# Six instead of three expert layers by seven products of quarters, with sums and copies in another order

## The chip, the core and the metric

The kernel runs on one core of a Trainium2 chip. A core has the engines PE (TensorE, matmul, with its weight loads as PEld), DVE (VectorE), ACT (ScalarE), POOL (GpSimd) and SP (SyncE, which only issues transfers here); sixteen DMA engines move data between HBM and SBUF. The metric is the time of one execution on the device, in microseconds. Each engine runs its own instructions in the order in which the program lists them.

## The reference

An attention with decay is followed by a mixture of experts in which a token may stick to its predecessor's expert. 8 batches of 576 tokens have 512 features; 8 experts have 1024 hidden features.

```python
def _attn_ref(q, k, v, f):
    scores = scale * np.matmul(q, k.transpose(0, 1, 3, 2))
    cum = np.cumsum(np.log(np.clip(f, 0.0001, 1.0)), axis=-1)
    scores = np.where(causal, -1000000000.0, scores + (cum[:, :, :, None] - cum[:, :, None, :]))
    attn = np.exp(scores - np.max(scores, axis=-1, keepdims=True))
    return np.matmul(attn / (np.sum(attn, axis=-1, keepdims=True) + 1e-09), v)
...
def _moe_ref(x, w_gate, w_local, w1, w2):
    logits = np.einsum('bsd,de->bse', x, w_gate)
    local_gate = 1.0 / (1.0 + np.exp(-np.einsum('bsd,de->bse', x, w_local).squeeze(-1)))
    for b in range(B):
        prev_e = -1
        for s in range(S):
            fresh_e = int(np.argmax(logits[b, s]))
            e = fresh_e if s == 0 or local_gate[b, s] < 0.5 else (prev_e if prev_e >= 0 else fresh_e)
            prev_e = e
            p = softmax(logits[b, s])
            out[b, s] = p[e] * (np.maximum(x[b, s] @ w1[e], 0.0) @ w2[e])
```

## The kernel before

The first 440 us are attention and routing, which the change leaves alone up to where the experts begin. Then each expert's tokens are gathered and the expert's two layers run over them. Two experts (0 and 1) are fixed and have run a part of their tokens by then; `fixed` runs their remainder of 256 and 320 tokens. Six more are *ranked* by their number of tokens, so that their rooms have fixed sizes of 608, 592, 576, 576, 544 and 480 tokens (`RANKC`), and `ranked` runs them one after the other. Which expert has which rank is known only on the chip, so its weights are loaded through a register.

All products are f16 in three parts: a value is cut into a high half (ACT, `uh`, `wh`, `hh`, `th`) and a low rest (DVE, `ul`, `wl`, `hl`, `tl`), and high x high, high x low and low x high are added up in PSUM. Cutting a ready tile is therefore one ACT and one DVE instruction (L2093, L2094). The hidden activations are cut in the ReLU itself: ACT writes `hh`, DVE writes `hl` from the same source and `hh`.

A **plain first layer** has 8 column blocks of 12 products, each in two halves of the tokens: 192 matmuls of n = tokens/2 columns (z, L1763), and per block one ReLU of all tokens on ACT (L1738) and its low part on DVE (L1739), both from PSUM.

A first layer **by sevens** (`seven`) splits the 512 input rows and the 1024 hidden columns into quarters of the weights and the tokens into halves, and forms the four blocks of the result from seven products of sums instead of eight. That is 28 products of 6 matmuls of n columns (L1848), 168 in all, in four groups g; a generator yields after each product. It needs the sums of quarters of the weights: POOL adds and subtracts f32 tiles (`add` L2117, `subtract` L2122, two times `less` L2131 for each half c of the rows, eight operations of 512 columns), and ACT and DVE cut the results (`second_row`, `differences`, `first_row`, each 1024 wide, `total` 512 wide, for both c). It needs sums of the token halves: `sums_of` makes them on DVE from the transposed tokens `xT` and cuts them (`part` and `cut`, L1908 to L1922). In the layer itself the products 1, 6 and 7 share one PSUM bank (`zb`), so ACT copies its state out after each (`kept`, L1855); DVE adds such a copy to another product (L1861), and ACT and DVE make the ReLU of the sum (L1863, L1864). The product after must wait for the copy before it overwrites the bank. In the last group the order is 1, 2, 4, 6, 5, 7, 3, 4, 3, where the first 4 and 3 belong to the group before.

A **second layer** has 24 products of 512 columns for each tile of 128 tokens (L1805, L1809); ACT scales the result (`put`, L1749) and POOL scatters it to `out` (L1751).

What stands beside these is a list `todo` of calls with step numbers: `run` issues each call after that step of the current expert (steps 0 to 27 are the products of a layer by sevens, or the half blocks of a plain one's 16, and four steps for each tile of the second layer follow). During expert r the list prepares expert r + 1: `load` (SP, 512 KB weight tiles into a ring of seven), gathers of tokens (POOL, L1695) and their transposes (SP, L1700), quarter sums, cuts, token sums. Before the change the second, fourth and sixth ranked expert go by sevens and are prepared during the first, third and fifth, which are plain and have 16 steps in the first layer (`SA`, `SB`, `LA`, `UA`, `TA`, `XA`); the plain ones are prepared beside layers by sevens (`XB`, `UB`, `PB`):

```python
                todo += [(16, free), (XA[0], both(*gs)), (XA[1], both(*ts))]
                for name, at in (SA if r < 4 else SB).items():
                    todo += [call(at[c], getattr(N, name), c) for c in C2]
                todo += [call(LA[2 * c + h], N.less, c, h) for c in C2 for h in C2]
                todo += [(TA[j], N.parts[j]) for j in range(4)]
                todo += [call(UA[j], N.second, j, None) for j in range(4)]
```

## Time and profile before

| | us |
|---|---|
| median of 3 runs | 782.54 (781.16 to 785.14) |
| the profiled execution | 784.0 |
| its span | 782.3 |
| busy: PE, PEld | 743.6, 542.0 |
| busy: DVE, ACT, POOL | 541.9, 477.0, 437.9 |
| mean granted clock | 0.993 |

The profile is of one execution. A window lists the busy time of each engine in a stretch with the number of its instructions, the granted clock as a share of full speed (1.00 is 2.4 GHz), and the share of DMA time. A group of instructions has a line of the program, an engine, an operation and its shape; then its count, its busy time in us, the mean of one in ns, and the engine's idle time before with what ended it. A time line lists an engine's instructions by their start in us and length in us; in brackets the idle time before it and the releaser.

### The profile page before, as it was taken

The page shows a single profiled execution, that of the slowest core. Times are in us where ns is not written, and L with a number is a line of the kernel's source. Part 1 is how long each engine was busy: PE and PEld are TensorE (multiplying, and loading weights), DVE is VectorE, ACT ScalarE, POOL GpSimd, SP SyncE. Part 2 cuts the span into 40 slices and gives each one's busy share as a digit, 9 for nine tenths or more (in the row PEclk, how much of TensorE's full clock was granted, in tenths as well). Part 3 has the DMA queues.
Part 4 walks back from the last instruction along what each step waited for, and adds up shares of the span by engine and source line. Part 5 has one row for each costly group of instructions (what it writes and reads, how often), then busy time and mean ns, then how long its engine had stood idle before and what let it go on. Part 6 is the DMA issues. An engine that isn't in the chain of part 4 may idle for free.

```text
span 782.3 us, 21826 instructions
## 1 busy us (share of the span) xinstructions
PE 743.6 (95%) x8733; PEld 542.0 (69%) x8733; DVE 541.9 (69%) x1211; ACT 477.0 (61%) x922; POOL 437.9 (56%) x497
## 2 busy tenths in 40 slices
PE   6898999999999998989799999999999999999996
PEld 3686888887778877877555576675665747476682
DVE  6886888898898989899758845166462574637440
ACT  7886788988878878868633334244463544525431
POOL 6879969395779859838692424181311924155101
PEclk9999999999999999999999999999999999999999
DMA  7569879698786868155794765939357293656101
GB/s 190 134 132 213 168 160 186 158 155 202 157 188 124 176 154 158 34 102 189 175 259 169 224 137 135 263 81 223 130 109 250 68 292 107 129 203 142 42 2 52
DMA packets 189659, 120.76 MB, mean 154 GB/s; under 512 B 129397, under 2 KB 165511, under 8 KB 189532
## 3 DMA queue, kind: packets, MB, share of 16 engines
q1 hardware_dynamic: 183473, 100.19, 55.1%
q0 software_dynamic: 6080, 19.13, 8.3%
q8 instruction: 70, 1.15, 0.6%
q14 instruction: 36, 0.29, 0.1%
HBM read 72.25 MB, written 19.32 MB: 117 GB/s over the span
## 4 chain that ended last, share of the span: by engine, by line
PE 65%; DVE 11%; issue 9%; ACT 6%; POOL 4%; DMA 3%; POOLq 1%; ACTq 0%; DVEq 0%
PE y L1805 17%; PE z L1763 12%; PE pt L940 8%; PE st L894 7%; PE xp L919 6%; DVE nm L905 4%; PE zb L1848 3%; PE st L429 3%; DVE pl L949 3%; ACT P L925 2%; ACT ph L945 2%; PE zd L1848 2%; POOLq L1750 1%; PE st L901 1%; PE y L1809 1%
## 5 line engine op out<-in xcount | busy, mean ns | idle before, releaser
L925 ACT ACTIVATE P<-st,nm 128x512 f32<-128x512 f32 (+3 forms) x288 | 152.8, 588 | 28.0 <-DVE nm L905 26.0
L905 DVE TENSOR_REDUCE nm<-st 128x1 f32<-128x512 f32 (+4 forms) x264 | 133.4, 542 | 8.0 <-PE st L901 5.5
L945 ACT CAST ph<-pt 128x512 f16<-128x512 f32 (+1 forms) x200 | 115.3, 587 | 35.3 <-PE pt L940 32.8
L940 PE MATMUL pt<-ident,P 128*128 128x128 f32 x784 | 121.0, 280 | 4.9 <-DVE pl L949 2.1
L949 DVE TENSOR_TENSOR pl<-pt,ph 128x512 f16<-128x512 f32 (+1 forms) x165 | 109.1, 669 | 22.6 <-ACT ph L945 20.8
L1751 POOL DMA_INDIRECT out_dram<-o,ranki x26 | 28.9, 1111 | 163.8 <-ACT o L1749 96.1
L1763 PE MATMUL z<-xT,wh 128*128 128x384 f16 (+5 forms) x640 | 117.8, 294 | 0.1
L1805 PE MATMUL y<-uh,hh 128*128 128x512 f16 x264 | 100.2, 379 | 0.0
L1805 PE MATMUL y<-uh,hl 128*128 128x512 f16 x264 | 100.2, 379 | 0.0
L1805 PE MATMUL y<-ul,hh 128*128 128x512 f16 x264 | 100.2, 379 | 0.0
L940 PEld LDWEIGHTS pt<-ident,P 128*128 128x128 f32 x784 | 83.8, 142 | 21.2 <-DVE pl L949 3.7
L919 PE MATMUL xp<-VH,pl 128*128 128x65 f16 (+1 forms) x960 | 89.2, 194 | 5.8 <-DVE pl L949 5.1
L919 PE MATMUL xp<-VH,ph 128*128 128x65 f16 (+1 forms) x960 | 90.8, 195 | 2.0 <-ACT ph L945 2.0
L1805 PEld LDWEIGHTS <-hh 128*128 128x128 f16 x528 | 51.3, 98 | 58.6
L919 PEld LDWEIGHTS <-ph 128*128 128x128 f16 (+1 forms) x1920 | 83.0, 102 | 10.4 <-issue 3.3
L919 PE MATMUL xp<-VL,ph 128*128 128x65 f16 (+1 forms) x960 | 90.2, 194 | 0.0
L1739 DVE SCALAR_TENSOR_TENSOR hl<-z,hh 128x384 f16<-128x384 f32 (+5 forms) x56 | 34.0, 611 | 75.2 <-ACT hh L1738 75.1
L894 PE MATMUL st<-Ak,Aq 128*128 128x256 f16 (+4 forms) x448 | 78.1, 285 | 4.4 <-ACT P L925 2.4
L894 PE MATMUL st<-KB,QB 70*128 70x256 f16 (+4 forms) x448 | 77.6, 282 | 2.0 <-DMA KB<-Ak 2.0
L919 PEld LDWEIGHTS <-pl 128*128 128x128 f16 (+1 forms) x960 | 74.7, 102 | 7.1 <-DVE pl L949 6.2
L1763 PE MATMUL z<-xT,wl 128*128 128x384 f16 (+5 forms) x320 | 78.5, 294 | 0.0
L1763 PEld LDWEIGHTS <-wh 128*128 128x128 f16 x640 | 61.9, 98 | 22.3 <-issue 0.7
(415 smaller groups left out, 1594.2 us busy)
## 6 DMA issues: line engine op xcount, KB each, us to landing
stg<-in_moe_w_dram SPq DMA_DIRECT2D x64, 512.0 KB
xs<-xr SPq DMA_DIRECT2D x16, 512.0 KB
ldq<-in_q_dram SPq DMA_DIRECT2D x14, 512.0 KB
ldk<-in_k_dram SPq DMA_DIRECT2D x14, 512.0 KB
ldv<-in_v_dram SPq DMA_DIRECT2D x28, 256.0 KB
QB<-Aq SPq DMA_DIRECT2D x15, 256.0 KB
KB<-Ak SPq DMA_DIRECT2D x15, 256.0 KB
ldv<-in_v_dram SPq DMA_DIRECT2D x20, 64.0 KB
```

What stands on the lines that cost most here:

```text
L894: nc.tensor.matmul(st[p0:p0 + m, co:co + n], lhsT=queries(lq, kk, h, c), rhs=rhs, start=(ps == 0 and first and co == col), stop=(ps == 1), ...
L905: nc.vector.tensor_reduce(dst, src, axis=AX.X, op=ALU.max, negate=True)
L919: nc.tensor.matmul(xo, lhsT=a[:, c0:c0 + m], rhs=w[:, vi, :], start=False, stop=(i == n - 1 and jj == 2), skip_group_check=True)
L925: nc.scalar.activation(P[:, c0:c1].rearrange("p (k x r) -> p k r x", r=2, x=64), st[:, c0:c1].rearrange("p (k r x) -> p k r x", r=2, x=64) ...
L940: nc.tensor.matmul(U["pt"][:, i * 128:(i + 1) * 128], lhsT=P[:, i * 128:(i + 1) * 128], rhs=ident, is_transpose=True, start=(i == 0), stop ...
L945: nc.scalar.copy(U["ph"][:, :cols], U["pt"][:, :cols])
L949: nc.vector.tensor_tensor(U["pl"][:, :cols], U["pt"][:, :cols], U["ph"][:, :cols], ALU.subtract)
L1739: nc.vector.scalar_tensor_tensor(lv, z[:, 0:nh, 0:wd], 0.0, hv, ALU.max, ALU.subtract)
L1751: nc.gpsimd.indirect_dma_start(out=outf if EX.get("over") else next_out(), out_offset=bass.IndirectOffsetOnAxis(ap=scat(t)[0:m], axis=0), ...
L1763: nc.tensor.matmul(z[:, a, 0:wd], lhsT=w[:, d, fc * 128:(fc + 1) * 128], rhs=xT[:, x, a * wd:(a + 1) * wd], start=(i == 0), stop=(i == len ...
L1805: nc.tensor.matmul(y[0:m], lhsT=a[:, fc, t * 128:t * 128 + m], rhs=u[:, fc], start=(i == 0), stop=(i == len(prods) - 1))
L1848: nc.tensor.matmul(out, lhsT=w, rhs=v, start=(start and i == 0), stop=(i == len(ops) - 1), skip_group_check=True)
```

## The change

All six ranked experts now have their first layer by sevens; there is no plain one left beyond the fixed experts. PE has 72 matmuls and as many weight loads less on its list. What prepares an expert is laid out anew, the same for each r. In the first layer of expert r stand the gathers (step 4), then the eight sums of quarters on POOL (steps 6 to 13), three of four pairs of cuts of expert r's own second-layer weights (`UC`, six high cuts on ACT and six low ones on DVE, 512 wide), the transposes (step 20) behind a load (`UN`, step 18). In its second layer stand all cuts of quarters (`WC`) and the token sums (`TA`) of the next expert, and at step 45 the first quarter of its second-layer weights (`UB`). The first ranked expert is prepared during the two fixed ones (`FA`). `sums_of` works on all four blocks of a half at once, in operations of 4n, 2n, n and n elements, and cuts 4n at once. In `seven` the ReLU of a sum is put off (`later`) behind the next product's copy. `less` writes to a new tile `s3` instead of the loaded weights. The first layer's quarters live in `wpa` alone; `wpb` and the freed halves of it hold the second layer's weights in turn; the pool `ov` goes, its tiles lie in rooms of `fx`. The core of the diff:

```diff
-SA = {"add": (2, 7), "subtract": (3, 8), "second_row": (4, 9), "differences": (10, 14), "first_row": (20, 22), "total": (24, 25)}
-SB = {**SA, "differences": (14, 18)}
...
+SEVEN = (1, 1, 1, 1, 1, 1)
+WP = (28, 30, 32, 36)
+LA = (6, 7, 8, 9), (10, 11, 12, 13)
+UC = (0, 1), (2, 3), (8, 10), (15, 17), (22, 23), (26, 27)
+UB = 45
+UN = (5, 18, 28)
+XA = (4, 20)
+WC = (28, 29, 29, 30, 31, 31, 38, 38)
+TA = (28, 36, 37, 44)
+FA = (9, 10, 11, 12, 13, 14, 15, 16), (17, 18, 19, 20), (1, 4, 7, 9), (17, 22), (15, 16, 17, 18), 22
...
-            return EX["fx"].tile([128, 304], F32, name="et", bufs=7)[:, 0:n]
+            return EX["fx"].tile([128, 304], F32, name="et", bufs=5)[:, 0:n]
...
-            nc.scalar.activation(hh[:, fc, half[h]], x, AF.Relu)
-            nc.vector.scalar_tensor_tensor(hl[:, fc, half[h]], x, 0.0, hh[:, fc, half[h]], ALU.max, ALU.subtract)
+
+            def finish():
+                nc.scalar.activation(hh[:, fc, half[h]], x, AF.Relu)
+                nc.vector.scalar_tensor_tensor(hl[:, fc, half[h]], x, 0.0, hh[:, fc, half[h]], ALU.max, ALU.subtract)
+
+            if plus is None:
+                finish()
+            else:
+                later.append(finish)
+
+        later = []
...
+            while len(later) > (p in (2, 3, 7)):
+                later.pop(0)()
...
+            if p == last[-1]:
+                for f in later:
+                    f()
...
-            x = [[EX["fx"].tile([128, 304], F32, name="et", bufs=7)[:, 0:n] for h in range(2)] for d in range(2)]
-            for d in range(2):
-                for h in range(2):
-                    y = slice(h * n, h * n + n)
-                    nc.vector.tensor_tensor(x[d][h], xT[:, 2 * d + c, y], xT[:, 4 + 2 * d + c, y], ALU.add)
-            (b11, b12), (b21, b22) = x
-            nc.vector.tensor_tensor(b11, b12, b11, ALU.subtract)
-            nc.vector.tensor_tensor(b12, b22, b12, ALU.subtract)
-            nc.vector.tensor_tensor(b22, b22, b11, ALU.subtract)
-            nc.vector.tensor_tensor(b21, b21, b22, ALU.subtract)
-            S_[c] = x
+            x = S_[c] = EX["fx"].tile([128, 2, 2, 304], F32, name="sx", bufs=1)[:, :, :, 0:n]
+            whole = [xT[:, i:i + 3:2, 0:2 * n].rearrange("p d (h x) -> p d h x", h=2) for i in (c, 4 + c)]
+            nc.vector.tensor_tensor(x, *whole, ALU.add)
+            flat = x.rearrange("p d h x -> p (d h) x")
+            nc.vector.tensor_tensor(flat[:, 0:2], flat[:, 1:4:2], flat[:, 0:2], ALU.subtract)
+            nc.vector.tensor_tensor(x[:, 1, 1], x[:, 1, 1], x[:, 0, 0], ALU.subtract)
+            nc.vector.tensor_tensor(x[:, 1, 0], x[:, 1, 0], x[:, 1, 1], ALU.subtract)
 
         def cut(c):
             x = S_.pop(c)
-            for d in range(2):
-                for h in range(2):
-                    y = slice(h * n, h * n + n)
-                    nc.scalar.copy(th[:, c, d, y], x[d][h])
-                    nc.vector.tensor_tensor(tl[:, c, d, y], x[d][h], th[:, c, d, y], ALU.subtract)
+            hi, lo = (t[:, c, :, 0:2 * n].rearrange("p d (h x) -> p d h x", h=2) for t in (th, tl))
+            nc.scalar.copy(hi, x)
+            nc.vector.tensor_tensor(lo, x, hi, ALU.subtract)
...
+        def second_room(self, r):
+            names, to = (("wh", "wl"), "p d (h m) -> p (d h) m") if r % 2 == 0 else (("uh", "ul"), "p (d h) m -> p (d h) m")
+            self.u = [EX["wpb"].tile([128, NF, DM] if r % 2 else [128, ND, FF], F16, name=x).rearrange(to, h=2) for x in names]
+
+        def second(self, j, c, low):
+            hi, lo = (x[:, 2 * j + c] for x in self.u)
+            t = self.ts[ND + j].rearrange("p (c m) -> p c m", c=2)[:, c]
+            if not low:
+                nc.scalar.activation(hi, t, AF.Copy, scale=WS)
+                return
+            nc.vector.scalar_tensor_tensor(lo, t, WS, hi, ALU.mult, ALU.subtract)
+            if c:
                 self.load()
 
...
+            def less(h):
+                if h == 0:
+                    self.s3[c] = EX["fx"].tile([128, 2, FF // 2], F32, name="s3", bufs=2)
+                nc.gpsimd.tensor_tensor(self.s3[c][:, h], b[:, h], self.s2[c], ALU.subtract)
+
+            return [add, subtract, lambda: less(0), lambda: less(1)]
...
+    todo = [(8, half_rows), (13, OV[1])]
+    todo += [(x, f) for x, f in zip(FA[0], [f for c in C2 for f in N.sums(c)])]
+    todo += [(FA[1][0], lambda: N.room(True))]
+    todo += [call(FA[1][2 * i + c], f, c) for i, f in enumerate((N.second_row, N.differences)) for c in C2]
+    X0 = []
+    todo += [(FA[3][0], lambda: X0.extend(tokens_of(0))), (FA[3][0], lambda: whole(both(*X0[1]))), (FA[3][1], lambda: whole(both(*X0[2])))]
+    fixed(0, W0, EX["x0"], *split_at(todo))
...
+        todo += [call(y, M.second, (i + 2) // 2, i % 2, low) for i, x in enumerate(UC) for low, y in enumerate(x)]
...
+            todo += [call(0, N.load, ST)] + [call(x, N.load) for x in UN]
+            todo += [(XA[0], both(*gs)), (XA[1], both(*ts))]
+            if SEVEN[r + 1]:
+                N.x, parts_ = sums_of(xn, RANKC[r + 1])
+                todo += [(LA[c][i], lambda N=N, c=c, i=i: N.sums(c)[i]()) for c in C2 for i in range(4)]
+                todo += [(WC[0], lambda N=N: [N.room(x) for x in (True, False)])]
+                todo += [(TA[0], parts_[0])]
+                todo += [call(WC[2 * i + c], f, c) for i, f in enumerate((N.first_row, N.second_row, N.total, N.differences)) for c in C2]
+                todo += list(zip(TA[1:], parts_[1:]))
...
+            todo += [call(UB, N.second_room, r + 1)] + [call(UB, N.second, 0, i // 2, i % 2) for i in range(4)]
```

What moves on DVE in the first layer of the fourth ranked expert (576 tokens), from the third group's last sum to the second sum of the last group (`et` are sums, `zd`, `yt`, `zb` PSUM banks, `ul` second-layer weights). Before:

```order
L1861 TENSOR_TENSOR et_12857<-zd_12787,et_12855 128x288
L1864 SCALAR_TENSOR_TENSOR hl_12645<-et_12857,hh_12644 128x288
L1861 TENSOR_TENSOR et_12878<-yt_12871,et_12869 128x288
L1864 SCALAR_TENSOR_TENSOR hl_12645<-et_12878,hh_12644 128x288
L1864 SCALAR_TENSOR_TENSOR hl_12645<-zb_12786,hh_12644 128x288
L1861 TENSOR_TENSOR et_12912<-zd_12862,et_12910 128x288
L1864 SCALAR_TENSOR_TENSOR hl_12645<-et_12912,hh_12644 128x288
```

and after:

```order
L1861 TENSOR_TENSOR et_12977<-zd_12851,et_12892 128x288
L1866 SCALAR_TENSOR_TENSOR hl_12772<-et_12977,hh_12771 128x288
L2120 SCALAR_TENSOR_TENSOR ul_12726<-stg_12553,uh_12725 128x512
L1861 TENSOR_TENSOR et_12996<-zd_12929,et_12994 128x288
L1866 SCALAR_TENSOR_TENSOR hl_12772<-et_12996,hh_12771 128x288
L1861 TENSOR_TENSOR et_13019<-yt_13012,et_13008 128x288
L1866 SCALAR_TENSOR_TENSOR hl_12772<-zb_12928,hh_12771 128x288
L1866 SCALAR_TENSOR_TENSOR hl_12772<-et_13019,hh_12771 128x288
L2120 SCALAR_TENSOR_TENSOR ul_12726<-stg_12731,uh_12725 128x512
```

The low ReLUs stand in almost the same order, and two low cuts of 512 columns stand between them. On ACT at the same place (copies `et<-zb`, ReLUs `hh`), before:

```order
L1855 COPY et_12869<-zb_12861 128x288
L1863 ACTIVATE hh_12644<-et_12878 128x288
L1863 ACTIVATE hh_12644<-zb_12786 128x288
L1855 COPY et_12896<-zb_12861 128x288
L1855 COPY et_12910<-zb_12861 128x288
L1863 ACTIVATE hh_12644<-et_12912 128x288
L1863 ACTIVATE hh_12644<-et_12922 128x288
```

and after:

```order
L1855 COPY et_13008<-zb_13000 128x288
L1865 ACTIVATE hh_12771<-et_12996 128x288
L1865 ACTIVATE hh_12771<-zb_12928 128x288
L1865 ACTIVATE hh_12771<-et_13019 128x288
L1855 COPY et_13042<-zb_13000 128x288
L2118 ACTIVATE uh_12725<-stg_12731 128x512
L1855 COPY et_13058<-zb_13000 128x288
```

The ReLU of a sum now follows the next copy, the ReLU straight from `zb` goes ahead of the sum's, and a high cut stands between two copies. On POOL in the first layer of the first ranked expert (`stg` are loaded weights, `xg` gathered tokens), before:

```order
L2117 TENSOR_TENSOR stg_10992<-stg_10992,stg_11004 128x512
L2122 TENSOR_TENSOR s2_11054<-stg_10992 128x512
L2131 TENSOR_TENSOR stg_11004<-stg_11004,s2_11054 128x512 x2
L2117 TENSOR_TENSOR stg_11006<-stg_11006,stg_11008 128x512
L2122 TENSOR_TENSOR s2_11130<-stg_11006 128x512
L2131 TENSOR_TENSOR stg_11008<-stg_11008,s2_11130 128x512 x2
L1695 DMA xg_11223<-xs_60,ranki_9851 128x1024
L1695 DMA xg_11225<-xs_60,ranki_9851 128x1024
L1695 DMA xg_11227<-xs_60,ranki_9851 128x1024
```

and after:

```order
L1695 DMA xg_11084<-xs_60,ranki_9851 128x1024
L1695 DMA xg_11086<-xs_60,ranki_9851 128x1024
L1695 DMA xg_11088<-xs_60,ranki_9851 128x1024
L1695 DMA xg_11090<-xs_60,ranki_9851 128x1024
L1695 DMA xg_11092<-xs_60,ranki_9851 80x1024
L2132 TENSOR_TENSOR stg_11028<-stg_11028,stg_11040 128x512
L2136 TENSOR_TENSOR s2_11128<-stg_11028 128x512
L2141 TENSOR_TENSOR s3_11139<-stg_11040,s2_11128 128x512 x2
L2132 TENSOR_TENSOR stg_11042<-stg_11042,stg_11044 128x512
```

The sums of quarters went ahead of the gathers and now follow them.

## Rows read from the trace of the kernel before

**Rows 1.** Windows: stretch, length, busy PE, PEld, DVE, ACT, POOL (instructions), granted clock, DMA share, GB/s.

```profile
503.68:528.49 24.81, 24.81 (x195) 18.76 (x193) 13.82 (x13) 10.88 (x14) 19.86 (x15) 1.00 0.39 107
528.49:553.73 25.24, 25.24 (x199) 13.91 (x197) 16.39 (x31) 11.72 (x20) 2.94 (x3) 1.00 0.86 219
...
599.51:623.03 23.52, 23.52 (x193) 18.74 (x192) 10.84 (x12) 10.71 (x14) 16.64 (x12) 1.00 0.29 103
623.03:646.59 23.56, 23.56 (x146) 11.82 (x144) 17.80 (x33) 11.67 (x20) 7.77 (x7) 1.00 0.93 275
646.59:667.25 20.66, 20.66 (x170) 16.42 (x169) 10.09 (x24) 9.85 (x26) 6.91 (x7) 1.00 0.28 86
...
690.81:713.06 22.25, 22.25 (x195) 18.75 (x193) 12.86 (x12) 9.56 (x13) 18.04 (x14) 1.00 0.32 109
```

**Rows 2.** Groups of instructions by form, 440 to 783 us: count | busy us, mean ns | idle before.

```profile
L2094 DVE SCALAR_TENSOR_TENSOR wl<-s,wh 128x512 f16<-128x512 f32 x6 | 3.9, 685 | 4.0 <-ACT wh L2093 4.0
L2094 DVE SCALAR_TENSOR_TENSOR ul<-stg,uh 128x1024 f16<-128x1024 f32 x20 | 24.3, 1245 | 1.7 <-ACT uh L2093 1.7
L1908 DVE TENSOR_TENSOR et<-xT 128x288 f32<-128x288 f16 x8 | 3.2, 453 | 2.5 <-DMA xT<-xg 2.5
L1864 DVE SCALAR_TENSOR_TENSOR hl<-et,hh 128x288 f16<-128x288 f32 x12 | 5.5, 458 | 6.1 <-ACT hh L1863 6.1
L2093 ACT ACTIVATE wh<-s 128x512 f16<-128x512 f32 x6 | 3.4, 621 | 0.0
L2093 ACT ACTIVATE uh<-stg 128x1024 f16<-128x1024 f32 x20 | 20.1, 1044 | 0.0
```

**Rows 3.** Time line of POOL, fifth ranked expert's first layer: start us, us, instruction.

```profile
695.59 1.30 POOL L2117 TENSOR_TENSOR stg<-stg 128x512 f32<-128x512 f32 x1
696.96 2.14 POOL L2122 TENSOR_TENSOR s<-stg 128x512 f32<-128x512 f32 x1
...
705.32 3.56 POOL L2131 TENSOR_TENSOR stg<-stg,s 128x512 f32<-128x512 f32 x2
```

**Rows 4.** Time line of DVE, the same layer; idle before and its releaser in brackets.

```profile
695.40 2.58 DVE L2094 SCALAR_TENSOR_TENSOR wl<-stg,wh 128x1024 f16<-128x1024 f32 x1 [0.22 <-ACT wh L2093]
...
700.96 1.81 DVE L2094 SCALAR_TENSOR_TENSOR wl<-stg,wh 128x1024 f16<-128x1024 f32 x1 [0.22 <-ACT wh L2093]
...
705.58 0.72 DVE L1739 SCALAR_TENSOR_TENSOR hl<-z,hh 128x544 f16<-128x544 f32 x1 [2.06 <-ACT hh L1738]
706.52 1.23 DVE L2094 SCALAR_TENSOR_TENSOR ul<-stg,uh 128x1024 f16<-128x1024 f32 x1 [0.22 <-ACT uh L2093]
```

**Rows 5.** Time line of ACT, second ranked expert's first layer, last group of sevens.

```profile
569.32 0.45 ACT L1863 ACTIVATE hh<-et 128x296 f16<-128x296 f32 x1 [0.53 <-DVE et L1861]
...
570.68 0.45 ACT L1863 ACTIVATE hh<-et 128x296 f16<-128x296 f32 x1 [0.62 <-DVE et L1861]
```

**Rows 6.** Time line of POOL, first, second and fourth ranked experts: start of sums or gathers.

```profile
507.83 1.28 POOL L2117 TENSOR_TENSOR stg<-stg 128x512 f32<-128x512 f32 x1
...
562.84 1.02 POOL L1695 DMA_INDIRECT xg<-xs,ranki  x1 [0.30 <-issue]
...
652.20 1.12 POOL L1695 DMA_INDIRECT xg<-xs,ranki  x1 [0.30 <-issue]
...
657.46 0.90 POOL L1695 DMA_INDIRECT xg<-xs,ranki  x1 [0.30 <-issue]
```

**Rows 7.** Time line of SP's queue, transposes in the first and third ranked expert.

```profile
525.33 11.33 SPq L1700 DMA_TRANSPOSE xT<-xg  x5
...
624.31 8.38 SPq L1700 DMA_TRANSPOSE xT<-xg  x5
```

**Rows 8.** Time line of DVE, token sums behind those transposes.

```profile
540.98 1.22 DVE L1908 TENSOR_TENSOR et<-xT 128x296 f32<-128x296 f16 x3 [0.32 <-DMA xT<-xg]
...
634.25 1.20 DVE L1908 TENSOR_TENSOR et<-xT 128x288 f32<-128x288 f16 x3 [1.41 <-DMA xT<-xg]
```

**Rows 9.** Time line of DVE, first operation of the first ranked expert.

```profile
507.70 0.79 DVE L1739 SCALAR_TENSOR_TENSOR hl<-z,hh 128x608 f16<-128x608 f32 x1 [16.06 <-ACT hh L1738]
```

More of the change, by code (lines that the diff above doesn't have):

```diff
@@ L1755, in experts @@
         if sums:
-            yield from seven(W, xT, sums, nt // 2, hh, hl)
+            yield from seven(W.w, xT, sums, nt // 2, hh, hl)
+        uh, ul = W.u if isinstance(W, Halves) else W[-2:]
         for fc in range(0 if sums else NF):
-            wh, wl = W[0:2]
+            wh, wl = (W.w if isinstance(W, Halves) else W)[0:2]
             z = products(0).tile([128, 2, 512], F32, name="z")
@@ L2326, in rank_loads @@
     def rank_loads():
[L2327 to L2329 removed]
+        N = EX["N"] = Halves(lambda: number(0))
+        N.load(7)
     def piece():
@@ new lines @@
+    X0 = []
+    todo += [(FA[3][0], lambda: X0.extend(tokens_of(0))), (FA[3][0], lambda: whole(both(*X0[1]))), (FA[3][1], lambda: whole(both(*X0[2])))]
+    fixed(0, W0, EX["x0"], *split_at(todo))
+    N.room(False)
+    xn = X0[0]
+    N.x, parts_ = sums_of(xn, RANKC[0])
+    todo = [call(FA[2][2 * i + c], f, c) for i, f in enumerate((N.first_row, N.total)) for c in C2]
+    todo += list(zip(FA[4], parts_))
+    todo += [call(FA[5], N.second_room, 0)] + [call(FA[5], N.second, 0, i // 2, i % 2) for i in range(4)]
@@ L2546 @@
+            todo += [call(UB, N.second_room, r + 1)] + [call(UB, N.second, 0, i // 2, i % 2) for i in range(4)]
+        if not SEVEN[r]:
+            todo = [(x - 12 if x > 27 else x * 16 // 28, f) for x, f in todo]
+        ranked(r, M, xc, M.x, *split_at(todo))
     mctx.close()
```

143 lines of the change are left out of this document (43 added, 100 removed).

## The prediction

> **What bounds the kernel now.** I read the table of windows first, cut at the first and last product of each layer of the ranked experts [rows 1]. In every window from the first ranked expert to the last, PE's busy time is the window's whole length at a granted clock of 1.00, so each product that is taken out shortens the run by its own length, as long as nothing else becomes late. The same rows give the room of the others: beside a plain first layer of 23.52 us DVE works 10.84 and ACT 10.71, but POOL 16.64; beside the second layer of 23.56 us DVE already works 17.80. Then I read the groups of instructions for the price of one cut or sum [rows 2], and the time lines of POOL, DVE, ACT and SP at the places where the change puts something new [rows 3 to 9].
>
> **First layers.** A plain first layer is 192 products, by sevens it is 168 of the same width, so 24 go in each of the first, third and fifth ranked experts (608, 576 and 544 tokens). One product is 24.81/192 = 0.129 us, 23.52/192 = 0.1225 and 22.25/192 = 0.116 [rows 1], so 24 of each are 3.1 + 2.9 + 2.8 = 8.8. The middle one can be read directly: 576 tokens take 23.52 us plain and 20.66 us by sevens, 2.86 less where the product's price gives 2.94; with all three scaled so it is 8.6. I take **8.7 us**. Weight loads for the remaining products are as many per product as before. Both sides of this price are in rows, so it needs no wider bounds.
>
> **What the second layers must now hold on DVE.** All cuts of quarters and the token sums of the next expert go there. For 576 tokens: a wide token sum is 4n, 2n, n and n elements with n = 288; from 685 ns for 512 and 1245 ns for 1024 elements [rows 2] an element is 1.09 ns over a base of 0.13, so 1.39 + 0.76 + 2 x 0.453 = 3.05, twice 6.1. Their two low cuts of 4n are 2.8, four quarter cuts of 1024 are 5.0, two of 512 are 1.4, two differences 2.5. That is 17.7, with hand-overs from ACT some 18.1 of 23.56 us. It fits as a sum, and PE does not wait for DVE's busy time but for the order: all of it stands behind the first token sum, which waits for the transposed tokens. Their way: the transposes now stand on SP behind a weight load that waits for the low cut of step 17, which ends some 14.8 us after the expert's start (17 of 28 products of 20.66/28 = 0.738 are 12.5, the third product of the group before, its ReLU and that cut follow). Allow 0.8 for the load's issue, an estimate, and add 8.4 for five transposes [rows 7], 1.6 to landing (624.31 + 8.38 = 632.69, and DVE's sums go on at 634.25) [rows 8], 18.1 of queue: 43.7. The first product that needs it is the third of the next expert, at 20.66 + 23.56 + 2 x 0.738 = 45.7. So 2.0 us are left in the third expert; the same sum gives 4.4 in the first (608 tokens), 3.0 and 2.0 in the second and fourth, and 4.0 before the last, which has 480 tokens and four transposes. I take **no stall**, since each margin is positive; if the landing is later it is the second rival.
>
> **POOL's sums beside a first layer by sevens.** This is where I see the price. Before, POOL's eight sums of quarters ran beside plain layers, ahead of the gathers; now they run behind the five gathers, beside layers by sevens, in which DVE has twelve low ReLUs that read two operands from SBUF (0.458 each) and six low cuts (0.685) [rows 2]. The rows of the fifth expert show what such a pair does [rows 3, 4]: DVE's cut that began at 695.40 took 2.58 us where an undisturbed one is 1.23 to 1.25, and POOL's sum at 695.59 ran its 1.30 in it; the next POOL sum at 696.96 took 2.14. The DVE cut at 700.96 took 1.81; the one at 706.52 took 1.23, and there POOL's two sums from 705.32 took 3.56 instead of 2.6. DVE's operation on PSUM at 705.58 took its usual 0.72 with POOL at work. So the two kinds go one after the other, and either may be the one that waits: DVE lost 1.36, 0.59 and 0.0, mean 0.65.
>
> The Trainium skill, SBUF — State Buffer, section "SBUF: two separate sides", says that VectorE and GpSimd share a port pair under an exclusive lock held for the whole instruction. That speaks against this change, and the trace agrees, with 2.58 us for a cut of 1.23; by this rule alone each of the three tight operations below would wait for the rest of a POOL sum in each of five experts. An estimate by it is 5 x (3 x 0.65 - 0.42) = 7.7 us in place of the 3.3 that follow from the rows.
>
> When do the sums run? POOL is free of the scatters and starts at 507.83, 4.1 us into the first expert, at 562.84, 9.1 into the second, at 652.20, 5.6 into the fourth, and five gathers take 6.2 (652.20 to 657.46 + 0.90) [rows 6]. The eight sums took 13.3 us in the fifth expert (695.59 to 705.32 + 3.56) [rows 3], so they run for about as long from 10.3, 15.3, 14.3 (third), 11.8 and 9.8 us into the five experts. What is tight there is the start of the last group of sevens. Counted for 576 tokens from the expert's start: low ReLU of the second group's last sum 13.7 to 14.2; low cut to 14.8; sum of the seventh product 14.7 to 15.2; its ReLU behind the next copy, 15.3 to 15.7; low ReLU to 16.2; next sum to 16.57; its ReLU; the copy that the seventh product, due at 24 x 0.738 = 17.7, waits for. The steps between are those of the second expert's rows: ACT's ReLU waits for DVE's sum and takes 0.45 [rows 5]. The sum may end as late as 16.9, so 0.34 are spare. With sums on POOL the first low ReLU and the cut lose 0.65 once between them (0.08 of that is spare), the next low ReLU 0.65 again: 1.22 less the 0.34 is 0.9 a piece in the first, fourth and fifth expert. In the second and third the sums begin only in time for the last wait: 0.65 less 0.34, 0.3 a piece. Together 3 x 0.9 + 2 x 0.3 = **3.3 us**. The ends: 0 if DVE wins each time, and 5 x (3 x 1.30 - 0.08 - 0.34) = 17.4 if all three operations wait for a whole sum in all five. I take 3.3 because the three rows' mean is half a POOL sum.
>
> **Edits with small prices.** Deferring a ReLU of a sum behind the next copy moves 0.45 us of ACT work and takes nothing away; before, ACT waited 0.53 and 0.62 us for DVE's sum ahead of these [rows 5], and the copy behind it could start only then. It can gain only where PE waits for that copy, and PE shows no wait: 0. The six high cuts of second-layer weights beside the first layer are 0.62 each on ACT [rows 2], 3.7 us added to 9.85 of 20.66 [rows 1], at 0; in the last expert one stands ahead of the last ReLU: 0.2. The first ranked expert is prepared beside the fixed experts: DVE stood idle there for 16.06 us up to 507.70 [rows 9], so its cuts and sums are hidden; on ACT the first tile's output may stand behind two cuts of 1.04 and one of 0.62 [rows 2], so 0 to 2.7, and I take 0.3, since the output tiles have two banks and the next tile's products run meanwhile. Narrower rooms (five sums' buffers for seven): a buffer is freed in the order in which the low ReLUs run, which are costed above. Sum 0.5.
>
> **Sum.** The profiled execution took 784.0, 1.46 above the median of 782.54. 784.0 - 8.7 + 3.3 + 0.5 = 779.1, and 1.46 less is **777.6**. PE has 72 products fewer on its list, so that the change does what it says is not in question.
>
> **Rival 1, slower.** POOL gets its turn after every DVE operation, so that all three of the tight operations wait in every one of the five experts. By 0.65 each, one POOL sum's half, that is 5 x (1.95 - 0.42) = 7.7, by whole sums 17.4; the middle is 12.5: 784.0 - 8.7 + 12.5 + 0.5 = 788.3, **786.8** on the median's scale. It decides the sign once the stalls pass 8.2 us, 1.6 per expert. For it: 2.58 us at 695.40, a wait for a whole sum. Against: 1.23 at 706.52 with POOL waiting instead [rows 3, 4]. Chance 0.19.
>
> **Rival 2, the tokens come late.** In the first ranked expert the transposes took 11.33 us from 525.33 and DVE's sums went on at 540.98 [rows 7, 8]: 15.7, where I use 8.4 + 1.6 = 10.0. With 5.6 us more the margins of 4.4, 3.0, 2.0, 2.0 and 4.0 become stalls of 1.2, 2.6, 3.6, 3.6 and, with four transposes, 0.5: 11.5 in all. What PE waits in the first layers would widen these margins, so it is not added: 784.0 - 8.7 + 11.5 + 0.5 = 787.3, **785.8**, no change. Against: those transposes ran beside weight loads that the new order issues elsewhere, and the others took 8.4. Chance 0.13.
>
> **Rival 3, no meeting of DVE and POOL in the tight places.** 784.0 - 8.7 + 0.5 = 775.8, **774.3**. For it: an operation that finds the way free loses nothing, and DVE is busy only half of the time. Against: POOL's sums stand back to back. Chance 0.23.
>
> **How the numbers follow.** The forecast has 0.45. It spreads from 775.5 to 780; a measurement tells some 0.5% from no change, so faster means under 778.6, slower over 786.5. Two thirds of the forecast lie under 778.6 (0.30), with rival 3 (0.23) and a little more for rival 2 at a part of its delay that is 0.54 faster. Slower is rival 1 at prices over 12.2 us, somewhat over half of it, and a third of rival 2, together 0.15. The rest, 0.31, is same: rival 2, the upper third of the forecast, the lower part of rival 1. The range leaves out 0.1 at each end: from 773.6, all of the 8.7 with none of the small prices, to 787.5, just past rival 1.
>
> **What the changed profile would show.** First layers of about 21.7, 20.7 and 19.5 us in the first, third and fifth expert if nothing stalls. PE idle ahead of the seventh product of the fourth group, released by ACT's copy, with a low ReLU on DVE of 0.9 to 1.7 instead of 0.46 a little before it, if the forecast or rival 1 is right. PE idle ahead of the third product of an expert, released by the token cuts, with transposes of over 10 us, if rival 2 is right. Second layers should stay at 25.2 and 23.6. The forecast fails in another way if PE waits in the second layers for a cut of the second-layer weights, or if the fixed experts' stages grow by more than 1 us.

## The result

Over 12 runs each the changed kernel took 788.9 us (784.33 to 790.67) and the kernel before 783.3 us (780.03 to 785.58): ratio 1.0067, interval 1.0043 to 1.0092, so some 5 us **slower**, where 777.6 was forecast. The profiled execution of the changed kernel took 788.54 us with a span of 786.6, against 784.0 and 782.3.

Page of the changed kernel, busy us by engine:

```profile
PE 736.1 (94%) x8661; PEld 535.4 (68%) x8661; DVE 613.7 (78%) x1295; ACT 509.9 (65%) x1006; POOL 474.8 (60%) x521
```

PE works 7.5 us less than before and the run is longer: PE now waits. Before, the whole expert part had one PE wait, of 0.66 us in the last expert. The same view, waits of PE from the first fixed expert on, of the changed kernel (waiter, releaser, us in total, times, longest):

```profile
PE zb L1848 <- ACT et L1855: 7.8, 7, 1.6
PE z L1763 <- DVE hl L1738: 2.7, 2, 2.3
PE zd L1848 <- DVE et L1861: 0.2, 1, 0.2
```

Windows of the changed kernel: the first fixed expert's first layer (10.48 us before), then the first layers of the first five ranked experts (columns as in rows 1):

```profile
457.92:471.45 13.53, 10.80 (x97) 9.39 (x96) 8.65 (x24) 3.29 (x8) 11.22 (x10) 1.00 0.25 31
508.33:531.20 22.87, 21.89 (x171) 16.39 (x169) 16.48 (x29) 13.49 (x33) 19.63 (x15) 1.00 0.77 253
556.43:579.05 22.62, 21.38 (x169) 16.43 (x168) 16.17 (x29) 13.52 (x33) 16.39 (x14) 1.00 0.79 261
603.65:626.01 22.36, 20.89 (x169) 16.42 (x168) 16.10 (x29) 13.22 (x33) 16.34 (x14) 1.00 0.80 266
649.57:672.51 22.94, 21.06 (x170) 16.43 (x169) 16.89 (x29) 13.01 (x33) 18.48 (x14) 1.00 0.81 244
696.07:718.44 22.37, 19.95 (x170) 16.43 (x169) 16.50 (x30) 12.86 (x33) 17.12 (x13) 1.00 0.73 246
```

Without waits the five layers by sevens last 21.71, 21.19, 20.58, 20.66 and 19.47 us (the first, third and fifth from e6 below, the second and fourth from the kernel before, which ran those two by sevens). So 1.16 + 1.43 + 1.78 + 2.28 + 2.90 = 9.55 us are lost in them, and 3.05 in the fixed expert's. PE's listed waits in the five are some 1.6 us less than 9.55, since its busy time also grows around a wait (21.89 against 21.71 in the first). All second layers are as long as before. The account from the fixed expert to the end: -8.82 (three layers by sevens instead of plain) + 9.55 + 3.05 - 1.14 (the last expert's first layer with the 96 matmuls behind it, 22.63 to 21.49, the wait of 0.66 before among it) = +2.6, and the two spans differ by 2.7 there. The other 1.6 us of the spans lie ahead of the fixed expert, in the first 40 us, at a granted clock of 0.91 against 1.00; that start lay between 453.3 and 460.7 us in the traces of this case and is no part of the change. The rest of the 5 us has the size of a longer wait in the fixed expert: in a second trace of the changed kernel (a0 below and last section) the stretch from there to the end is 332.0 us, where b0, the kernel before beside it, has 326.3. How many runs wait so long is not known.

Where the wait comes from shows in the fourth expert, last two groups of sevens. POOL of the changed kernel, sums of quarters:

```profile
658.95 1.28 POOL L2132 TENSOR_TENSOR stg<-stg 128x512 f32<-128x512 f32 x1
660.30 1.61 POOL L2136 TENSOR_TENSOR s<-stg 128x512 f32<-128x512 f32 x1
662.00 2.81 POOL L2141 TENSOR_TENSOR s<-stg,s 128x512 f32<-128x512 f32 x2
664.76 1.49 POOL L2132 TENSOR_TENSOR stg<-stg 128x512 f32<-128x512 f32 x1
666.33 1.60 POOL L2136 TENSOR_TENSOR s<-stg 128x512 f32<-128x512 f32 x1
```

and DVE beside it, where a low cut (L2120) and the low ReLU of a sum (L1866, `hl<-et,hh`) have both operands in SBUF:

```profile
651.69 0.68 DVE L2120 SCALAR_TENSOR_TENSOR ul<-stg,uh 128x512 f16<-128x512 f32 x1
...
658.47 2.31 DVE L2120 SCALAR_TENSOR_TENSOR ul<-stg,uh 128x512 f16<-128x512 f32 x1
660.71 0.44 DVE L1861 TENSOR_TENSOR et<-zd,et 128x288 f32<-128x288 f32 x1
661.66 0.57 DVE L1866 SCALAR_TENSOR_TENSOR hl<-et,hh 128x288 f16<-128x288 f32 x1 [0.51 <-ACT hh L1865]
...
664.55 0.57 DVE L1866 SCALAR_TENSOR_TENSOR hl<-et,hh 128x288 f16<-128x288 f32 x1 [0.51 <-ACT hh L1865]
665.04 1.76 DVE L2120 SCALAR_TENSOR_TENSOR ul<-stg,uh 128x512 f16<-128x512 f32 x1
666.72 0.45 DVE L1861 TENSOR_TENSOR et<-zd,et 128x288 f32<-128x288 f32 x1
...
669.94 1.42 DVE L2120 SCALAR_TENSOR_TENSOR ul<-stg,uh 128x512 f16<-128x512 f32 x1 [0.25 <-ACT uh L2118]
```

A low cut takes 0.68 us before POOL's sums begin and 2.31, 1.76 and 1.42 among them; a low ReLU takes 0.57 instead of 0.46. The difference between the two is how much of POOL's sum is left when they come. The cut at 665.04 follows a low ReLU at once: POOL has taken its turn between the two, and the cut waits for the rest of that sum. The low ReLU at 661.66 comes 0.9 us after the cut's end, when POOL's sum is nearly through, and waits 0.1. The distance to the operation ahead counts only because POOL's sums stand back to back here, and the next one gets its turn as DVE's operation ends. Where a sum has just begun for another reason, a low ReLU loses nearly as much though it comes 1.05 us after the cut ahead of it. This is the first meeting in the first ranked expert:

```profile
519.17 1.28 POOL L2132 TENSOR_TENSOR stg<-stg 128x512 f32<-128x512 f32 x1
519.41 1.38 DVE L1866 SCALAR_TENSOR_TENSOR hl<-et,hh 128x304 f16<-128x304 f32 x1 [0.60 <-ACT hh L1865]
```

The price of a cut is then the whole chain's: the sum at 666.72 stands behind it, ACT's ReLU behind the sum, the copy behind the ReLU, and PE waits 1.44 us for the copy. By the Trainium skill, SBUF — State Buffer, section "SBUF: two separate sides", whichever of the two starts first keeps the ports for its whole instruction. Most rows agree with that: DVE's operations waited for the rest of the sum that ran as they came, and POOL's sums of 1.6 us instead of 1.28 waited for DVE. They add that the turns alternate while both stand ready. One row does not fit as it is listed: the cut at 658.47 began 0.48 us ahead of the sum at 658.95, while POOL still issued its last gather, and yet waited to the end of that sum, so it lost 1.63, more than a sum. The cut at 695.40 in rows 4 is of the same kind: it began 0.19 us ahead of the sum at 695.59 and lost 1.36.

### The profile page after: what moved, and what is told of

The parts are those of the page before. It is cut to its first block, busy times and chain, and to the rows that moved or that the text cites. A ratio compares the mean times of both kernels' runs of the same rounds, so it can differ in the third digit from the quotient of the medians.

```text
span 786.6 us, 21919 instructions
## 1 busy us (share of the span) xinstructions
PE 736.1 (94%) x8661; PEld 535.4 (68%) x8661; DVE 613.7 (78%) x1295; ACT 509.9 (65%) x1006; POOL 474.8 (60%) x521
## 4 chain that ended last, share of the span: by engine, by line
PE 54%; DVE 15%; issue 12%; POOL 8%; ACT 7%; POOLq 2%; DMA 0%; SPq 0%; ACTq 0%; DVEq 0%
PE y L1805 15%; PE pt L940 8%; PE st L894 6%; PE z L1763 6%; PE xp L919 5%; PE zb L1848 4%; DVE nm L905 3%; DVE pl L949 3%; PE st L429 2%; POOLq L1749 2%; ACT ph L945 2%; ACT P L925 2%; PE zd L1848 2%; DVE hl L1866 1%; POOL s L2141 1%
## 5 line engine op out<-in xcount | busy, mean ns | idle before, releaser
L1750 POOL DMA_INDIRECT out_dram<-o,ranki x26 | 34.4, 1323 | 134.7 <-ACT o L1748 102.6
L919 PEld LDWEIGHTS <-ph 128*128 128x128 f16 (+1 forms) x1920 | 82.9, 102 | 10.3 <-issue 3.0
L1805 PE MATMUL y<-uh,hh 128*128 128x512 f16 x168 | 63.7, 379 | 0.0
L1805 PE MATMUL y<-ul,hh 128*128 128x512 f16 x168 | 63.7, 379 | 0.0
L1805 PE MATMUL y<-uh,hl 128*128 128x512 f16 x168 | 63.7, 379 | 0.0
L1763 PE MATMUL z<-xT,wh 128*128 128x384 f16 (+2 forms) x256 | 55.1, 306 | 3.4 <-DVE hl L1738 3.2
L1866 DVE SCALAR_TENSOR_TENSOR hl<-et,hh 128x288 f16<-128x288 f32 (+4 forms) x72 | 40.0, 555 | 23.3 <-ACT hh L1865 21.6
L1865 ACT ACTIVATE hh<-et 128x288 f16<-128x288 f32 (+4 forms) x72 | 31.4, 436 | 30.0 <-DVE et L1861 29.7
L1848 PEld LDWEIGHTS <-wh 128*128 128x128 f16 x384 | 37.5, 98 | 18.2 <-issue 9.8
```

The costliest lines, as they stand in the source:

```text
L919: nc.tensor.matmul(xo, lhsT=a[:, c0:c0 + m], rhs=w[:, vi, :], start=False, stop=(i == n - 1 and jj == 2), skip_group_check=True)
L1750: nc.gpsimd.indirect_dma_start(out=outf if EX.get("over") else next_out(), out_offset=bass.IndirectOffsetOnAxis(ap=scat(t)[0:m], axis=0), ...
L1763: nc.tensor.matmul(z[:, a, 0:wd], lhsT=w[:, d, fc * 128:(fc + 1) * 128], rhs=xT[:, x, a * wd:(a + 1) * wd], start=(i == 0), stop=(i == len ...
L1805: nc.tensor.matmul(y[0:m], lhsT=a[:, fc, t * 128:t * 128 + m], rhs=u[:, fc], start=(i == 0), stop=(i == len(prods) - 1))
L1848: nc.tensor.matmul(out, lhsT=w, rhs=v, start=(start and i == 0), stop=(i == len(ops) - 1), skip_group_check=True)
L1866: nc.vector.scalar_tensor_tensor(hl[:, fc, half[h]], x, 0.0, hh[:, fc, half[h]], ALU.max, ALU.subtract)
```

## The experiments

The theories: **A**, POOL's sums and DVE's operations in SBUF shut each other out; **B**, ACT's queue is too full. Ratios are to the kernel before, run on the same chip in the same group of runs. e1 to e4 ran in one group, b0, a0, e5 and e6 in a second, e7 to e10 in a third.

**e1_no_sums**, POOL's sums left out:

```diff
-            return [add, subtract, lambda: less(0), lambda: less(1)]
+            self.s2[c], self.s3[c] = a[:, 1], b
+            return [lambda: None] * 4
```

> The changed kernel without POOL's sums of quarters for any ranked expert; the cuts read the loaded quarters instead, so the sums are left out of the computation and nothing else. Theory A (POOL's sums and DVE's operations with operands in SBUF shut each other out): the five first layers that took 22.87, 22.62, 22.36, 22.94 and 22.37 us go to 21.7, 21.2, 20.7, 20.7 and 19.5, and the first fixed expert's from 13.53 to 10.5, together 12.5 us less, about 776.5 us. Theory B (ACT's queue is too full: six high cuts and the ReLUs that were put off stand ahead of the copy for which PE waits): the five first layers keep their 113.2 us, the time stays within 1 us of 788.9 but for the fixed expert.

Ratio 0.9881 (0.9796 to 0.9966): some 14.5 us less than the change (1.0067). The fourth and fifth expert's windows:

```profile
657.67:678.26 20.59, 20.59 (x170) 16.45 (x169) 13.45 (x30) 13.33 (x33) 6.93 (x6) 1.00 0.88 274
701.82:721.29 19.47, 19.47 (x171) 16.45 (x170) 12.98 (x30) 13.13 (x33) 5.66 (x5) 1.00 0.85 285
```

No wait is left in these two, with the same six high cuts and put-off ReLUs on ACT: in these two A holds and B falls. The first three did not reach their 21.7, 21.2 and 20.7 in this trace (22.98, 25.13, 23.00), nor the fixed expert its 10.5 (15.58); there ACT stood without a semaphore to wait for, as in these two lines, so this trace tells nothing of them (e5 and e6 below do):

```profile
571.39 0.45 ACT L1865 ACTIVATE hh<-et 128x296 f16<-128x296 f32 x1 [1.65 <-issue]
573.81 0.71 ACT L1855 COPY et<-zb 128x296 f32<-128x296 f32 x2 [1.98 <-remote]
```

**e2_lows_early**, the cuts of a first layer moved ahead:

```diff
-UC = (0, 1), (2, 3), (8, 10), (15, 17), (22, 23), (26, 27)
+UC = (0, 1), (2, 3), (5, 6), (8, 10), (10, 11), (12, 13)
```

> The changed kernel with the pairs of cuts of second-layer weights of the third group and later moved to the first half of the first layer (steps 5 to 13 instead of 8 to 27), same work on every engine, POOL's sums unchanged. Theory A with the low cuts as the ones that lose (each waits for a whole POOL sum, since POOL gets the ports between two DVE operations that follow each other): the stalls of 9.5 us in the five first layers fall to 1 to 3 us, what the low ReLUs' 0.1 us waits leave, so 780 to 782 us. Theory A with the low ReLUs as the ones that lose: under 2 us less. Theory B: the six high cuts now crowd ACT in the first groups, stalls of the same size or more there, no gain.

Ratio 1.0054 (1.0016 to 1.0093), no gain: a miss, and the most instructive one. The last cuts came later than their steps say, into POOL's sums, and now close to each other. DVE of e2, fourth expert, from 9 us after its start:

```profile
665.18 2.13 DVE L2120 SCALAR_TENSOR_TENSOR ul<-stg,uh 128x512 f16<-128x512 f32 x1
667.24 0.44 DVE L1861 TENSOR_TENSOR et<-zd,et 128x288 f32<-128x288 f32 x1
667.61 1.39 DVE L2120 SCALAR_TENSOR_TENSOR ul<-stg,uh 128x512 f16<-128x512 f32 x1
668.92 1.51 DVE L1866 SCALAR_TENSOR_TENSOR hl<-et,hh 128x288 f16<-128x288 f32 x1
670.35 0.45 DVE L1861 TENSOR_TENSOR et<-yt,et 128x288 f32<-128x288 f32 x1
670.72 1.38 DVE L2120 SCALAR_TENSOR_TENSOR ul<-stg,uh 128x512 f16<-128x512 f32 x1
```

Low ReLUs also lose most of a sum when they follow a cut at once (1.51). PE's longest wait here, 1.93 us, has moved to the third group. So the kind of operation does not decide it: an operation loses what is left of the sum that runs as it comes. In the second and third expert no cut met a sum, but their layers have waits without a releaser (2.15 us on ACT in the second, 1.18 on PE in the third), so they tell nothing of the cuts.

**e3_fixed_small_ops**, the small operations in the first fixed expert moved behind POOL's sums:

```diff
-    todo = [(8, half_rows), (13, OV[1])]
+    todo = [(19, half_rows), (21, OV[1])]
```

> The changed kernel with the small DVE operations on half rows and on the overflow's tile numbers moved from steps 8 and 13 of the first fixed expert to steps 19 and 21, behind POOL's sums. Theory A: the first fixed expert's first layer goes from 13.53 to 10.5 to 10.7 us, the rest stays, so 3 us less: about 786. Rival (the low ReLUs there wait by themselves for the sums, whatever stands between): the layer keeps more than 12.5 us.

The layer is back at its time before, and the ratio is 1.0013 (0.9979 to 1.0048):

```profile
458.58:469.06 10.48, 10.48 (x98) 9.40 (x96) 3.24 (x9) 3.29 (x8) 8.16 (x8) 1.00 0.45 72
```

What stood there in the changed kernel, DVE's operations of 8 elements, 0.17 us each when alone:

```profile
465.65 1.20 DVE L2410 TENSOR_SCALAR nov<-nov 128x8 f32<-128x8 f32 x1
466.88 1.19 DVE L1363 TENSOR_SCALAR nov<-nov 128x8 f32<-128x8 f32 x1
468.11 0.17 DVE L1365 TENSOR_SCALAR nov<-nov 128x8 f32<-128x8 f32 x1
...
468.32 1.11 DVE L2414 TENSOR_TENSOR_SCAN ctl<-one,nov 128x8 f32<-128x8 f32 x1
```

Three of the four waited for one of POOL's sums; the one at 468.11 came 0.02 us ahead of POOL's next sum and took its 0.17. The low ReLUs of the plain layer stood behind them on DVE, and PE had no free bank for 2.25 us.

**e4_no_later**, ReLUs of sums at once again:

```diff
-            if plus is None:
-                finish()
-            else:
-                later.append(finish)
+            finish()
```

> The changed kernel with each ReLU of a sum issued at once again, ahead of the next product's copy, as in the kernel before. Theory A: the copies that PE waits for stand behind one more wait for DVE, so the stalls stay or grow, by up to 0.5 us a group where POOL's sums run: 789 to 793. Theory B (putting off costs): 3 to 5 us less.

Ratio 1.0231 (1.0148 to 1.0314), some 13 us more than the change: the direction of A, and three times the size expected. A copy that stands behind a ReLU waits for DVE's sum, which waits for the cut, which waits for POOL (in the third expert ACT stands 3.36 us ahead of such a ReLU, and PE then waits 2.69 for the copy).

**b0_before** and **a0_after**, the two kernels beside e5 and e6:

> The kernel before, unchanged, for its trace beside the experiments' traces. In three of the experiments' traces ACT or DVE stood 0.9 to 2.5 us in first layers with no semaphore to wait for, at a DMA share of 0.7 to 0.97; if that belongs to the chip, it also shows here; if it belongs to the weight loads that the change moved into first layers, the first layers here have no such wait and last 24.8, 21.2, 23.5, 20.7 and 22.3 us as in rows 1.

> The changed kernel, unchanged, beside the others of this call. Theory A: first layers as in its first trace (22.9, 22.6, 22.4, 22.9, 22.4) with PE's wait of 1.0 to 1.6 us ahead of the seventh product of the last group, and the ratio to the kernel before within 1.003 and 1.012.

b0's first layers were 24.81, 21.19, 23.52, 20.67 and 22.25 and had no wait without a releaser; a0's were 22.86, 22.62, 22.36, 22.93 and 22.35, within 0.02 of the first trace, ratio 1.0039 (1.0012 to 1.0065). So the stalls belong to the program. The waits without a releaser were absent from both; no trace of the kernel before was taken in the group of e1 to e4, so whether the loads that the change has moved into first layers (DMA share 0.7 to 0.8 against 0.3 [rows 1]) take part in them there stays open.

**e5_lows_ahead**, e3's edit, and all low cuts ahead of POOL's sums (the second quarter of the second-layer weights is cut in the second layer before):

```diff
-UC = (0, 1), (2, 3), (8, 10), (15, 17), (22, 23), (26, 27)
-UN = (5, 18, 28)
+UC = (0, 1), (2, 3), (5, 6), (8, 8)
+UN = (5, 9, 28)
...
-[call(UB, N.second, 0, i // 2, i % 2) for i in range(4)]
+[call(UB, N.second, j, c, low) for j in C2 for c in C2 for low in C2]
```

> The changed kernel with the second quarter of the second-layer weights cut in the second layer before (as the first already is) and the last four pairs of cuts at steps 0 to 8, so that all low cuts of a first layer end before POOL's sums begin (9.4 us and later); and the small operations of the fixed expert behind POOL's sums. Theory A in the form that the traces now suggest (POOL takes the ports between two DVE operations with operands in SBUF, so that one that follows another closely waits for a whole sum, one that comes 1 us later for 0.1): the five first layers come within 0.5 us each of 21.7, 21.2, 20.7, 20.7 and 19.5, the first fixed expert's first layer to 10.5; 10 to 12 us less than the changed kernel, ratio to the kernel before 0.990 to 0.995. Rival (the low ReLUs alone are enough to stall): first layers still over 22 us, ratio over 1.000.

Ratio 0.9894 (0.9856 to 0.9932), 776.6 us beside 783.5. The five first layers:

```profile
504.93:526.64 21.71, 21.71 (x170) 16.41 (x169) 13.88 (x28) 13.18 (x32) 15.45 (x13) 1.00 1.01 292
551.88:573.02 21.14, 21.14 (x170) 16.44 (x169) 13.70 (x29) 13.24 (x32) 13.71 (x12) 1.00 0.96 288
597.61:618.19 20.58, 20.58 (x169) 16.44 (x168) 13.73 (x29) 13.22 (x32) 13.19 (x12) 1.00 0.98 295
641.75:662.63 20.88, 20.75 (x170) 16.44 (x169) 14.16 (x29) 12.72 (x32) 18.16 (x15) 1.00 1.11 291
686.19:706.78 20.59, 19.83 (x171) 16.43 (x170) 14.23 (x29) 12.23 (x32) 16.76 (x13) 1.00 1.03 287
```

POOL's eight sums still run beside the sevens here. With only low ReLUs left among them, about one per POOL sum, PE waits 0.76 us once (fifth expert, whose last cut still met a sum and took 2.06). A part of this is not the edit's own doing: in the first three experts the sums also begin 1.4 to 3.1 us later than in the changed kernel. In the fourth and fifth they begin where they did (9.3 and 7.7 us into the expert), and there the layers fell by 2.06 and 1.78. Distance alone does not make a low ReLU cheap here either: the one at 526.01 came 2.5 us after the last, met a sum that began at 525.93 and took 1.51, but PE did not need it soon. In the second fixed expert's second layer ACT's new cuts cost 1.06.

**e6_every_other**, `SEVEN = (1, 0, 1, 0, 1, 0)`: sevens in the first, third and fifth expert, and POOL's sums beside plain layers as before:

> The changed kernel with only the first, third and fifth ranked expert by sevens, so that POOL's sums stand beside plain first layers again and none beside sevens; all else of the new layout stays (wide token sums, put-off ReLUs, six low cuts in each first layer of sevens). Theory A: the first layers by sevens last 21.7, 20.7 and 19.5 without a wait of PE, the first fixed expert keeps its 13.5. Theory B (the layout, ACT's queue or the low cuts stall the sevens by themselves): waits of 1 us and more in these three layers stay.

Ratio 1.0017 (0.9989 to 1.0045), with the fixed expert's 13.63. The first, third and fifth expert:

```profile
507.97:529.68 21.71, 21.71 (x171) 16.41 (x170) 14.03 (x30) 13.73 (x33) 8.00 (x7) 1.00 0.82 267
...
603.67:624.25 20.58, 20.58 (x169) 16.44 (x168) 13.40 (x30) 13.56 (x33) 5.85 (x6) 1.00 0.81 247
...
694.89:714.36 19.47, 19.47 (x170) 16.45 (x169) 12.89 (x30) 12.97 (x33) 5.65 (x5) 1.00 0.79 254
```

The new layout itself, with six cuts in the layer and DMA at 0.8, costs the sevens nothing. Only the meeting with POOL's sums does.

**e7_lows_ahead2**, e5 with that cut four steps later (`FA[5] + 4 * j`):

> As e5_lows_ahead, but the first ranked expert's second quarter of second-layer weights is cut four steps later in the second fixed expert, so that ACT's output of the second tile no longer stands behind it (PE waited 1.06 us for it in e5). Theory A: the second fixed expert's second layer goes from 14.3 to 13.2 us, the rest as in e5: ratio to the kernel before 0.985 to 0.993. Rival: ACT is full there anyway and the wait only moves: no change against e5.

The second layer is back at 13.19; ratio 0.9883 (0.9844 to 0.9921), not to be told from e5. Its trace again has waits of ACT without a releaser, up to 2.95 us, and its five first layers sum to 113.1 us where e5 has 104.9.

**e8_no_later2**, e4's edit on e7:

> e7 with each ReLU of a sum issued at once again. In e4, where the low cuts stood among POOL's sums, that cost about 10 us in the five first layers. If putting off matters only together with these waits, it is worth under 2 us here (first layers within 0.4 us of e7's); if ACT's copies need it whatever POOL does (they then wait for DVE's sum ahead of them), each first layer grows by 1 to 2 us also here, 5 to 10 in all.

Ratio 1.0074 (1.0041 to 1.0106). The five first layers sum to 124.6 us against 113.1 in e7: putting the ReLUs off is worth some 11.5 us also where the cuts stand ahead, more than the 5 to 10 of the second case. The size is rough, since both traces have waits without a releaser, and the fifth layer of e8 a granted clock of 0.87. The last expert, in which POOL has no sums, has none of these waits: its first layer took 18.36 us where it is 17.32 in e7. So a part of the gain needs no POOL.

**e9_narrow_sums**, e7 with the token sums in pieces of n elements:

> e7 with the token sums and their cuts in pieces of n elements again, as in the kernel before. By the durations 16 pieces more on DVE at some 0.13 us of base each are 2 us more in each second layer, inside a margin of 4: no change of the time (within 0.3% of e7). Rival: the margin is smaller than that, PE waits ahead of the third product of the next expert, 1 us or more each, 0.5% or more.

Ratio 0.9892 (0.9824 to 0.9959): no difference from e7 that can be told, though the interval is wider than the 0.3% that was expected. In its trace no wait of PE is released by a token cut, so the rival's sign is absent.

**e10_sums_first**, the sums ahead of the gathers as in the kernel before:

```diff
-LA = (6, 7, 8, 9), (10, 11, 12, 13)
+LA = (1, 1, 2, 2), (2, 2, 3, 3)
```

> The changed kernel with POOL's sums ahead of the gathers again, as in the kernel before. Theory A: the sums now meet the first three groups of sevens instead of the last; the wait ahead of the seventh product of the last group goes in the first, fourth and fifth expert, waits of about the same size come in the second and third group; and the tokens come some 6 us later than now, when DVE's last token cut ended 4.3 us ahead of its first reader (646.77 against 651.05), so PE also waits 1 to 3 us ahead of the third product of each next expert: 790 to 800. Rival (only the last group is tight): 780 to 785.

Ratio 1.0283 (1.0232 to 1.0334), beyond the worst expected. Waits of PE:

```profile
PE y L1805 <- ACT o L1748: 16.5, 4, 7.4
PE zb L1848 <- ACT et L1855: 6.8, 7, 1.4
```

The sums waited for their weights (4.76 us in the third expert), so they still met the last group, and the gathers and transposes came after them. The late tokens then hit earlier in the program than I had said: not the next expert's third product, but the second layer, where ACT's output of a tile stands behind the token cut that waits for DVE (11.47 us idle ahead of it) and PE runs out of banks.

## Why the prediction was wrong

**Right.** The gain of the first layers, 8.7: measured 8.82. That no second layer stalls: a wide token sum took 1.36 + 0.76 + 0.46 + 0.46 = 3.04 where 3.05 was worked out, and DVE's last token cut in the third expert ended 4.3 us ahead of its first reader, where 2.0 were estimated. The place: PE does wait ahead of the seventh product of the fourth group, released by ACT's copy, in each of the five experts.

**The step that failed** is the price of POOL's sums, 3.3 us, in place of which 9.55 was measured. Two things in it were wrong.

The first is when the sums run. They began 10.8, 12.1, 11.9, 9.4 and 7.8 us into the five experts, where 10.3, 15.3, 14.3, 11.8 and 9.8 were worked out, because POOL began the gathers ahead of them 5.7 us into the second expert and 2.2 into the fourth, where 9.1 and 5.6 were taken from the kernel before [rows 6]. So in the second and third expert, priced at 0.3 each, they met the whole tight place, and 1.43 and 1.78 were lost. In the fourth and fifth they also met a cut of the third group (2.31 us at 658.47, 1.75 at 705.38), PE waited there too, and 2.28 and 2.90 were lost where 0.9 was priced.

The second is the price of one meeting. It let "the first low ReLU and the cut lose 0.65 once between them", that is, it took DVE to keep the ports from one operation to the next, and took the mean of three rows for each wait. But an operation waits for what is left of POOL's sum, and those three rows [rows 4] show it: the sum that ran as the cut came, or began just behind it, ended 1.49, 0.72 and 0.07 us after the cut's start, and the cuts lost 1.36, 0.59 and 0.0. A cut right behind a low ReLU lost 1.07 to 1.63 (1.75 and 2.31 for 0.68), a low ReLU 0.9 us after another 0.1. At the tight place of the first expert the three operations lost 1.28 together, where the working had 0.65 twice: that this sum agrees is luck. What it left out is that the lateness of the group before is carried on. Beside e6 the low ReLU ahead of the tight cut already ended 0.53 us late in the first expert and 0.85 in the third.

That is rival 1's mechanism, all three operations waiting in all five experts, for which 7.7 to 17.4 were worked out and 0.19 was given, though the waits are not equal as it had them. The estimate by the Trainium skill, SBUF — State Buffer, section "SBUF: two separate sides", 7.7, was nearer than the sum by the mean of the rows.

**The term that was missing** is the first fixed expert, 3.05 us where the whole stage had 0.3. I priced ACT's place in the second fixed expert and DVE's idle time there, and did not look at what the small operations `half_rows` and `OV[1]` meet in the first one, although the diff puts `OV[1]` at step 13 and POOL's first sums at steps 9 to 16. It is the same mechanism with operations that nobody would count as work. The prediction did name a growth of the fixed experts' stages by more than 1 us as another way to fail.

**Two small ones.** Putting the ReLUs off was priced at 0 by the kernel before, in which PE never waited for the copies; in the changed kernel it is worth over 10 us (e4, e8), so without it the change would have lost over three times as much. The last expert got 1.1 us shorter instead of 0.2 longer; with the ReLUs at once again its first layer is 18.03 and 18.36 us (e4, e8) instead of 17.32, so it is the putting off that shortens it.

The sum with the measured terms is the +2.6 us of the account above, within the interval of a0 and just under that of the first 12 runs. Rival 2 did not occur in the changed kernel: its transposes took 6.1 to 8.5 us. In e10, where the sums keep their place, the tokens do come late, but because the gathers stand behind the sums and not by slow transposes.

## What to carry over

When a step moves to another place, list for every engine which operations of others shut it out there, small operations too, and look at when they meet: beside POOL's sums a DVE operation with its operands in SBUF costs what is left of the sum that runs as it comes. That was 0.1 us near its end and over 1 us near its start, and among sums that stand back to back an operation right behind another mostly meets the start. A mean over a few collisions is no price, and a step that moves also moves the time at which others begin. The gain was there all along: with the cuts ahead of POOL's sums and the small operations behind them the same six layers by sevens run 1.1% faster than the kernel before.
